# Scaling V's result instead of the probabilities in the first two attention chunks

## The chip, the cores and the metric

The kernel runs on one core of one Trainium2 chip. The metric is device time in microseconds (us) of one execution; a run is one timed execution. Three runs of the kernel before are shown, and one further execution was profiled.

## The reference

```python
scores = scale * np.matmul(q, k.transpose(0, 1, 3, 2))          # 4 batches, 8 heads, 768 positions, 64 per head
scores = scores - slope[h] * dist                               # distance bias; kept: 96 local keys, 8 global keys
scores = np.where(keep, scores, -1000000000.0)
a = np.exp(scores - np.max(scores, axis=-1, keepdims=True))
a = a / (np.sum(a, axis=-1, keepdims=True) + 1e-09)
x = np.matmul(a, v)                                             # heads side by side: 3072 tokens x 512
h = x @ w_in                                                    # 512 x 2048
g = 0.5 * h * (1.0 + erf(h / sqrt(2)))
out = g @ w_out                                                 # 2048 x 512
```

The weights come as 64-bit numbers, which the kernel takes apart itself.

## The kernel before

The 3072 tokens are 12 chunks `c` of 256 queries, three to a batch. A chunk first goes through the attention, 8 heads in 4 pairs `p`, then through 8 steps `s` of the two layers (256 of the 2048 inner columns each). Chunks 0 and 1 are interleaved: step 0 of chunk 0, three empty steps, then step 0 of chunk 1, step 1 of chunk 0, step 1 of chunk 1 and so on, while the weights of each step are still coming in; from chunk 2 on (`CAT`) the chunks follow each other. The list `EVENTS` says, for each chunk, at which step of the loop in `run` each part of its attention is written.

The attention of a pair of heads: `scores_pair` multiplies queries by keys on TensorE (tiles `s`) and VectorE adds the bias and finds the maximum (L358, tiles `n`); `exps` takes the exponential on ScalarE with the sum of each row (L379, `su`), VectorE adds 1e-9 and forms the reciprocal (L381, L382), and the probabilities are multiplied by it (L388; VectorE in chunks 0 and 1, GpSimd later). `flip` turns each head's probabilities by three transposes on TensorE (L398, tiles `t`), and ScalarE copies them to SBUF (L402, `pt`). `av_pair` multiplies by V (L430, `av`: per pair in chunk 0, per two pairs in chunk 1). The result goes to the tile `x` as a high part, a copy by ScalarE (L470, L475), and a low part, the rest, by VectorE (`lo_dve`, L177).

The layers: `m1` makes `h` (L506 for chunks 0 and 1; L489, L493, L495 later, with a sum of two halves on VectorE, L497). `gelu` reads it twice on ScalarE (`gh`, `gr`, L516, L517), and VectorE forms `gl` (L177). `m2` adds 12 products to `acc` (L536). The weights of a step are four pieces of 512 KB; each goes through ScalarE twice (L209, L229) and VectorE four times (L215, L217, L219, L177). In `run`, a step's `m1` stands ahead of the `m2` of the step before. `flag` gathers small checks near the end; it ends in a product on TensorE (L641, `flag_ps`) that waits for VectorE (`bad`, L639).

The exponential and the gelu need different function tables; a change of table is an `ACT_TABLE_LOAD` on ScalarE. `FILL` puts products with zeros (`warm`, L366) between the scores of chunks 0 and 1. The order on each engine is not that of the source: a scheduler, which follows data, buffers and the extra dependencies of `after`, lays the instructions out when the program is built, and each engine works through its list from the front.

Of the kernel before, what the change touches and what calls it, by code (L numbers as in the profile page):

```python
# [7 lines left out]
F32 = mybir.dt.float32  # L8
# [5 lines left out]
ALU = mybir.AluOpType  # L14
# [3 lines left out]
P = 128  # L18
# [3 lines left out]
NP = H // 2  # L22
# [19 lines left out]
EVENTS = [EVF, EVF, EVT] + [EVS] * (NCH - 3)  # L42
# [10 lines left out]
FILL = {(0, 0, 0): 8, (0, 0, 1): 5, (0, 1, 1): 9, (0, 2, 1): 4, (0, 3, 1): 4, (1, 0, 1): 4}  # L53
# [33 lines left out]
class Fast:  # L87
    def __init__(self, tc, ctx, qT, kT, v, w, out, limits):
# [22 lines left out]
        self.pt_n, self.pt_t, self.x = {}, {}, {}  # L111
# [4 lines left out]
    def consts(self):  # L116
# [3 lines left out]
        self.nmax = const.tile([P, 3 * NP + 1, 4], F32, name="nmax")  # L120
        self.qsc = const.tile([P, NP], F32, name="qsc")
# [198 lines left out]
    def scores_pair(self, c, p):  # L320
# [4 lines left out]
        su = self.sm.tile([P, 4], F32, name=f"su{c}_{p}", tag="su", bufs=4, padded_shape=[P, 8])  # L325
# [3 lines left out]
        prev = self.last_av if EVENTS[c] is not EVF else None  # L329
# [33 lines left out]

    def warm(self, n, prev=None):
# [7 lines left out]
    def exps(self, c, p):  # L372
# [9 lines left out]
        nc.vector.reciprocal(out=su, in_=su)  # L382
        if c >= 3:
            top = self.nmax[:, 3 * NP]
            nc.vector.tensor_tensor(out=top, in0=top, in1=mn, op=ALU.max)
        for nn, i in every:
            eng = nc.vector if c < 2 else nc.gpsimd
            ins = eng.tensor_scalar(out=nn, in0=nn, scalar1=su[:, i:i + 1], scalar2=0.0,  # L388
                                    op0=ALU.mult, op1=ALU.add)
        if c < 2:  # L390
            self.last_dve = ins.ins

    def flip(self, c, h):
        nc = self.nc
        nn = self.pt_n.pop((c, h))
        tp = self.bank([P, 3, P], f"t{c}_{h}")
        for i, o in enumerate((0, 2 * P, NK if c % CPB == 0 else P)):
            nc.tensor.transpose(tp[:, i, :], nn[:, o:o + P], self.ident)  # L398
# [6 lines left out]
    def av_pair(self, c, p):  # L405
# [15 lines left out]
        elif first:  # L421
            avb = self.bank([P, 2, n, P], f"av{c}_{p}")
            av = [avb[:, j] for j in range(2)]
        else:
            av = [self.bank([P, n, P], f"av{c}_{p}_{j}") for j in range(2)]
# [34 lines left out]
        if quarters:  # L460
# [6 lines left out]
            return  # L467
        if first:
# [9 lines left out]
    def m1(self, t, f):  # L478
# [5 lines left out]
        if c >= CAT:  # L484
# [3 lines left out]
            for d in range(NP):  # L488
# [3 lines left out]
                if d:  # L492
                    nc.tensor.matmul(hp[:, 0, :], lhsT=wl[:, d - 1, fs], rhs=x[:, d - 1, 0, :],  # L493
                                     start=False, stop=False, skip_group_check=True)
            nc.tensor.matmul(hp[:, 0, :], lhsT=wl[:, NP - 1, fs], rhs=x[:, NP - 1, 0, :],  # L495
                             start=False, stop=True, skip_group_check=True)
# [24 lines left out]
    def m2(self, t, k):  # L521
# [12 lines left out]
        for f in range(2):  # L534
            for g, w in ((gh, wh), (gh, wl), (gl, wh)):
                nc.tensor.matmul(acc, lhsT=g[:, f, ks], rhs=w[:, f, :],  # L536
                                 start=s == 0 and n == 0, stop=s == NST - 1 and n == 5)
# [284 lines left out]
```

## Time and profile before

| | us |
|---|---|
| three runs | 682.39, 683.29, 683.58 |
| median | 683.29 |
| the profiled execution's own time | 682.04 |
| its span (first to last instruction) | 680.2 |
| TensorE busy in the span | 665.6 |
| VectorE, ScalarE, GpSimd busy | 390.3, 364.6, 102.4 |

In the tables of rows, PE is TensorE's products and PEld its weight loads, DVE is VectorE, ACT ScalarE, POOL GpSimd. Names read as output<-inputs; tile numbers are left out there, so `t` is every `t0_0`, `t0_1` and so on (chunk, then head). A busy time of pipelined instructions includes the time that the last result takes to come out, so the spacing of starts tells the rate better.

### The profile page before, as it was taken

How to read it: one execution, taken by the hardware profiler on the slowest of the kernel's cores; microseconds unless marked ns; L12 is line 12 of the kernel's file. 1: busy time of each engine (PE TensorE's matmuls, PEld its weight loads, DVE VectorE, ACT ScalarE, POOL GpSimd, SP SyncE). 2: the span in 40 equal slices, each digit the busy share in tenths (PEclk: the TensorE clock that was granted, in tenths of full speed). 3: DMA queues.
4: the chain of work that ended last, by engine and by line, in shares of the span. 5: the costliest groups of instructions: out<-in, count | busy, mean ns of one | idle time of the engine just before them, and what ended most of it. 6: DMA issues, size and time to landing. Idle time of an engine off the chain costs nothing.

```text
span 680.2 us, 13571 instructions
## 1 busy us (share of the span) xinstructions
PE 665.6 (98%) x5215; PEld 561.5 (83%) x5215; DVE 390.3 (57%) x1136; ACT 364.6 (54%) x852; POOL 102.4 (15%) x232
## 2 busy tenths in 40 slices
PE   8989999999999999999999999999999999999996
PEld 6658898988888888888888888888888888888784
DVE  5989989334555654655555555555546555453432
ACT  3796687554654645536636537446456356363211
POOL 3100330310301301301201121031031031010000
PEclk9999999999999999999999999999999999999998
DMA  8945944241531613403514324224154052000001
GB/s 267 276 147 186 290 152 125 79 125 47 164 94 62 164 35 122 140 29 113 126 41 153 97 67 156 69 72 140 32 132 135 24 161 64 32 1 16 16 1 36
DMA packets 66183, 71.21 MB, mean 105 GB/s; under 512 B 32704, under 2 KB 49344, under 8 KB 66112
## 3 DMA queue, kind: packets, MB, share of 16 engines
q1 hardware_dynamic: 61664, 62.93, 30.6%
q10 hardware_dynamic: 4448, 7.34, 3.1%
q8 instruction: 43, 0.70, 0.4%
q14 instruction: 28, 0.23, 0.1%
HBM read 63.97 MB, written 6.29 MB: 103 GB/s over the span
## 4 chain that ended last, share of the span: by engine, by line
PE 94%; DVE 3%; ACT 2%; issue 0%; DVEq 0%
PE acc L536 40%; PE h L489 22%; PE h L493 8%; PE h L506 6%; PE av L430 5%; PE s L347 5%; PE t L398 4%; PE h L495 3%; PE warm_ps L366 1%; DVE n L358 1%; DVE n L388 1%; ACT w L209 0%; ACT n L379 0%; DVE wb L217 0%; ACT L516 0%
## 5 line engine op out<-in xcount | busy, mean ns | idle before, releaser
L489 PE MATMUL h<-x,winh 128*128 128x512 f32 x640 | 216.3, 400 | 0.0
L497 DVE TENSOR_REDUCE hs<-h 128x256 f32<-128x512 f32 x160 | 107.7, 685 | 99.5 <-PE h L495 98.9
L536 PE MATMUL acc<-wouth,gh 128*128 128x512 f32 x384 | 156.8, 408 | 2.2 <-ACT gh L516 2.2
L536 PE MATMUL acc<-woutl,gh 128*128 128x512 f32 x384 | 150.3, 392 | 0.0
L536 PE MATMUL acc<-wouth,gl 128*128 128x512 f32 x384 | 148.5, 393 | 0.1
L388 POOL TENSOR_SCALAR n<-n,su 128x192 f32<-128x192 f32 (+1 forms) x160 | 71.3, 464 | 438.3 <-ACT n L379 217.9
L177 DVE TENSOR_TENSOR gl<-gr,gh 128x512 fp32r<-128x512 f32 x96 | 67.5, 703 | 117.6 <-ACT gr L517 117.6
L493 PE MATMUL h<-x,winl 128*128 128x256 f32 x480 | 134.7, 281 | 0.0
L489 PEld LDWEIGHTS h<-x,winh 128*128 128x128 f32 x640 | 114.2, 188 | 20.4 <-issue 0.3
L516 ACT ACTIVATE gh<-hs 128x512 fp32r<-128x512 f32 x80 | 50.7, 633 | 125.6 <-DVE hs L497 122.1
L402 ACT COPY pt<-t 128x384 f32<-128x384 f32 x96 | 45.4, 479 | 112.8 <-PE t L398 109.5
L493 PEld LDWEIGHTS h<-x,winl 128*128 128x128 f32 x480 | 90.4, 188 | 7.2
L536 PEld LDWEIGHTS acc<-wouth,gh 128*128 128x128 f32 x384 | 72.2, 188 | 21.0 <-ACT xs L462 3.9
L536 PEld LDWEIGHTS acc<-wouth,gl 128*128 128x128 f32 x384 | 72.1, 188 | 17.0 <-issue 0.6
L536 PEld LDWEIGHTS acc<-woutl,gh 128*128 128x128 f32 x384 | 72.3, 188 | 12.3
L379 ACT ACTIVATE n<-n,mn 128x192 f32<-128x192 f32 (+1 forms) x144 | 62.3, 434 | 1.4 <-DVE mn L358 1.2
L358 DVE CUSTOM_DVE_ANT_0 n<-s,pen 128x192 f32<-128x192 f32 (+1 forms) x192 | 54.6, 340 | 2.2 <-PE s L347 2.2
L517 ACT ACTIVATE gr<-hs 128x512 f32<-128x512 f32 x80 | 49.3, 616 | 0.0
L506 PE MATMUL h<-x,winh 128*128 128x256 f32 x256 | 48.9, 286 | 0.4 <-ACT x L470 0.2
L398 PE MATMUL t<-ident,n 128*128 128x128 f32 x288 | 47.2, 274 | 1.2 <-DVE n L388 1.2
L430 PE MATMUL av<-pt,vr 64*64 64x64 f32 (+2 forms) x1312 | 42.8, 249 | 2.7 <-ACT pt L402 2.6
L495 PE MATMUL h<-x,winl 128*128 128x256 f32 x160 | 45.2, 282 | 0.0
(87 smaller groups left out, 738.2 us busy)
## 6 DMA issues: line engine op xcount, KB each, us to landing
w<-w SPq DMA_DIRECT2D x32, 512.0 KB, 5.0
c<-w SPq DMA_DIRECT2D x32, 512.0 KB, 5.3
out<-o ACTq DMA_DIRECT2D x23, 256.0 KB, 2.0
qr<-qT SPq DMA_DIRECT2D x11, 512.0 KB, 3.9
vr<-v SPq DMA_DIRECT2D x22, 256.0 KB, 4.2
kr<-kT SPq DMA_DIRECT2D x16, 320.0 KB, 5.0
vr<-v SPq DMA_DIRECT2D x19, 192.0 KB, 2.8
kr<-kT SPq DMA_DIRECT2D x36, 64.0 KB, 4.1
```

The costliest lines, as they stand in the source:

```text
L177: return self.nc.vector.tensor_tensor(out=out, in0=in_, in1=hi.bitcast(F32), op=ALU.subtract)
L358: ins = nc.vector.tensor_tensor_reduce(out=nn[:, j * NK:j * NK + n], in0=sp[hh][:, j, 0:n], in1=pen, scale=-slope(2 * p + hh), scalar=3e38 ...
L379: self.table(nc.scalar.activation(out=nn, in_=nn, func=AF.Exp, bias=mn[:, i:i + 1], scale=-1.0, accum_out=su[:, i:i + 1]))
L388: ins = eng.tensor_scalar(out=nn, in0=nn, scalar1=su[:, i:i + 1], scalar2=0.0, op0=ALU.mult, op1=ALU.add)
L398: nc.tensor.transpose(tp[:, i, :], nn[:, o:o + P], self.ident)
L430: ins = nc.tensor.matmul(out, lhsT=lhs, rhs=rhs, start=start, stop=stop, skip_group_check=True).ins
L489: nc.tensor.matmul(hp.rearrange("p e t -> p (e t)"), lhsT=wh[:, d, fs], rhs=x[:, d].rearrange("p e t -> p (e t)"), start=d == 0, stop=d == ...
L493: nc.tensor.matmul(hp[:, 0, :], lhsT=wl[:, d - 1, fs], rhs=x[:, d - 1, 0, :], start=False, stop=False, skip_group_check=True)
L495: nc.tensor.matmul(hp[:, 0, :], lhsT=wl[:, NP - 1, fs], rhs=x[:, NP - 1, 0, :], start=False, stop=True, skip_group_check=True)
L497: self.last_dve = nc.vector.tensor_reduce(out=self.h[t][:, f, :], in_=hp.rearrange("p e t -> p t e"), axis=mybir.AxisListType.X, op=ALU.ad ...
L506: nc.tensor.matmul(hp[:, f, :], lhsT=w[:, d, fs], rhs=x[:, d, e, :], start=n == 0, stop=n == 3 * NP - 1)
L536: nc.tensor.matmul(acc, lhsT=g[:, f, ks], rhs=w[:, f, :], start=s == 0 and n == 0, stop=s == NST - 1 and n == 5)
```

## The change

In chunks 0 and 1 the probabilities are no longer multiplied by the reciprocals. The transposes take the bare exponentials. After V's products, TensorE spreads the reciprocals of each head over that head's 64 rows: products of a reciprocal column, read 64 times, with the unit matrix (tile `r`, L490 of the changed file; four products of 64x128 for a pair of heads, 16 in each of the two chunks). ScalarE copies V's result out (`xs`), VectorE multiplies it by `r`, and then the high and low parts are made as before, from SBUF. V's products of chunk 0 are written one loop step later for pairs 0 to 2. `FILL` has 8 products of 512 columns fewer, and `FILL_T` adds two of 384 columns ahead of the transposes of head 6 of chunk 1. From chunk 3 on, a step's second layer has to stand behind the first layer of the next step.

```diff
@@ -39,7 +39,7 @@
-EVENTS = [EVF, EVF, EVT] + [EVS] * (NCH - 3)
+EVENTS = [EVF | {"av": (3, 4, 5, 5)}, EVF, EVT] + [EVS] * (NCH - 3)
...
-FILL = {(0, 0, 0): 8, (0, 0, 1): 5, (0, 1, 1): 9, (0, 2, 1): 4, (0, 3, 1): 4, (1, 0, 1): 4}
+FILL = {(0, 0, 0): 8, (0, 0, 1): 5, (0, 1, 1): 3, (0, 2, 1): 3, (0, 3, 1): 3, (1, 0, 1): 4}
+FILL_T = {(1, 6): 2}
+FILL_AV = {}
...
+        self.sums = const.tile([P, 2 * NP, 4], F32, name="sums")
...
-        su = self.sm.tile([P, 4], F32, name=f"su{c}_{p}", tag="su", bufs=4, padded_shape=[P, 8])
+        su = self.sums[:, c * NP + p] if c < 2 else self.sm.tile([P, 4], F32, name=f"su{c}_{p}", tag="su", bufs=4,
+                                                                 padded_shape=[P, 8])
...
-        prev = self.last_av if EVENTS[c] is not EVF else None
+        prev = self.last_av if c >= CAT else None
...
+    def zeros(self, n, out):
+        prev = self.last_t
+        for i in range(n):
+            ins = self.nc.tensor.matmul(out, lhsT=self.wz[:, 0:P], rhs=self.wz[:, 0:out.shape[1]],
+                                        start=True, stop=True, skip_group_check=True).ins
+            self.after(ins, prev, "behind the transposes of the head before")
+            prev = ins
...
         nc.vector.tensor_scalar(out=su, in0=su, scalar1=1e-9, scalar2=None, op0=ALU.add)
-        nc.vector.reciprocal(out=su, in_=su)
+        self.last_dve = nc.vector.reciprocal(out=su, in_=su).ins if c < 2 else self.last_dve
+        if c >= 2:
+            nc.vector.reciprocal(out=su, in_=su)
         if c >= 3:
             top = self.nmax[:, 3 * NP]
             nc.vector.tensor_tensor(out=top, in0=top, in1=mn, op=ALU.max)
+        if c < 2:
+            self.inv[c, p] = su
+            return
         for nn, i in every:
-            eng = nc.vector if c < 2 else nc.gpsimd
-            ins = eng.tensor_scalar(out=nn, in0=nn, scalar1=su[:, i:i + 1], scalar2=0.0,
-                                    op0=ALU.mult, op1=ALU.add)
-        if c < 2:
-            self.last_dve = ins.ins
+            nc.gpsimd.tensor_scalar(out=nn, in0=nn, scalar1=su[:, i:i + 1], scalar2=0.0, op0=ALU.mult, op1=ALU.add)
...
         tp = self.bank([P, 3, P], f"t{c}_{h}")
+        if (c, h) in FILL_T:
+            self.zeros(FILL_T[c, h], tp.rearrange("k i q -> k (i q)"))
         for i, o in enumerate((0, 2 * P, NK if c % CPB == 0 else P)):
-            nc.tensor.transpose(tp[:, i, :], nn[:, o:o + P], self.ident)
+            self.last_t = nc.tensor.transpose(tp[:, i, :], nn[:, o:o + P], self.ident).ins
...
+        if c < 2:
+            rb = self.bank([P, 2, n, P], f"r{c}_{p}")
+            for i, q in enumerate(ps):
+                su = self.inv.pop((c, q))
+                for j, hh in ((0, 0), (0, 1), (1, 0), (1, 1)):
+                    ins = nc.tensor.matmul(rb[hh * D:(hh + 1) * D, j, i, :], lhsT=dap(su, 2 * hh + j, [su.ap[0], [0, D]]),
+                                           rhs=self.ident, start=True, stop=True, skip_group_check=True).ins
+                    self.after(ins, self.last_av, "heads and halves in turn")
+                    self.last_av = ins
+            for j in range(n):
+                src, scale = (avb, rb) if first else (av[j], rb[:, j])
+                shape = [P, 2, n, P] if first else [P, n, P]
+                xs = self.pp.tile(shape, F32, name=f"xs{c}_{p}_{j}", tag="n")
+                if first:
+                    xh, xl = (self.x[c][:, ps.start:ps.stop, e].rearrange("d p (j q) -> d j p q", j=2) for e in range(2))
+                else:
+                    xh, xl = (self.x[c][:, ps.start:ps.stop, e, j * P:(j + 1) * P] for e in range(2))
+                nc.scalar.copy(xs, src)
+                nc.vector.tensor_tensor(out=xs, in0=scale, in1=xs, op=ALU.mult)
+                nc.scalar.copy(xh, xs)
+                self.lo_dve(xl, xs, xh)
+            return
...
-            nc.tensor.matmul(hp[:, 0, :], lhsT=wl[:, NP - 1, fs], rhs=x[:, NP - 1, 0, :],
-                             start=False, stop=True, skip_group_check=True)
+            self.last_m1 = t, nc.tensor.matmul(hp[:, 0, :], lhsT=wl[:, NP - 1, fs], rhs=x[:, NP - 1, 0, :],
+                                               start=False, stop=True, skip_group_check=True).ins
...
         for f in range(2):
             for g, w in ((gh, wh), (gh, wl), (gl, wh)):
-                nc.tensor.matmul(acc, lhsT=g[:, f, ks], rhs=w[:, f, :],
-                                 start=s == 0 and n == 0, stop=s == NST - 1 and n == 5)
+                ins = nc.tensor.matmul(acc, lhsT=g[:, f, ks], rhs=w[:, f, :],
+                                       start=s == 0 and n == 0, stop=s == NST - 1 and n == 5).ins
+                if n == 0 and c > CAT and self.last_m1[0] == t + 1:
+                    self.after(ins, self.last_m1[1], "behind the first layer of the next step")
                 n += 1
```

The lists of the engines change in three places that matter for what follows. In names such as `pt1_6` the first number is the chunk and the second the head; the last number is the buffer's.

The first place is ScalarE, from the second reading of chunk 0's first `h` (`gr0`) to the copies of the last transposed heads of chunk 1. Before:

```order
L379 ACTIVATE n1_5_629,su1_2_615<-n1_5_629,nmax_129 128x192 x2
L209 ACTIVATE w1_1_200<-w1_1_200 128x512
L402 COPY pt1_2_653<-t1_2_649 128x384
L402 COPY pt1_2_653<-t1_3_655 128x384
L229 CAST winh1_563<-wb1_0_568 128x512
L379 ACTIVATE n1_6_701,su1_3_690<-n1_6_701,nmax_129 128x192 x2
L379 ACTIVATE n1_7_704,su1_3_690<-n1_7_704,nmax_129 128x192 x2
L209 ACTIVATE w1_2_202<-w1_2_202 128x512
L402 COPY pt1_4_742<-t1_4_738 128x384
L475 CAST x1_614<-av1_1_0_660 128x2x128
```

And now:

```order
L212 ACTIVATE w1_1_201<-w1_1_201 128x512
L417 COPY pt1_2_643<-t1_3_645 128x384
L232 CAST winh1_558<-wb1_0_563 128x512
L502 COPY xs1_1_0_685<-av1_1_0_650 128x256
L502 COPY xs1_1_1_690<-av1_1_1_651 128x256
L504 CAST x1_609<-xs1_1_0_685 128x2x128
L504 CAST x1_609<-xs1_1_1_690 128x2x128
L417 COPY pt1_4_742<-t1_4_738 128x384
L391 ACTIVATE n1_6_705,sums_130<-n1_6_705,nmax_129 128x192
L417 COPY pt1_4_742<-t1_5_744 128x384
L391 ACTIVATE n1_6_705,sums_130<-n1_6_705,nmax_129 128x192
L391 ACTIVATE n1_7_708,sums_130<-n1_7_708,nmax_129 128x192 x2
```

The copies and casts of `x1`'s first half stood behind the exponentials of heads 6 and 7, and now stand ahead of them; one copy of `pt1_2` has moved ahead of `gr0`. Behind these exponentials both lists still have five weight pieces (`winh1`, `w1_2`, `w1_3`, `w2_0`, `w2_1`) ahead of the last copies, those of `pt1_6`.

The second place is TensorE, from the transposes of head 7 of chunk 1 to the first layer. Before:

```order
L398 MATMUL t1_7_776<-ident_132,n1_7_704 128x128 x2
L430 MATMUL av1_3_0_781<-pt1_4_742,vr1_191 64x128
L430 MATMUL av1_3_1_782<-pt1_4_742,vr1_191 64x128 x2
L506 MATMUL h4_827<-x1_614,winh0_322 128x256 x2
...
L506 MATMUL h5_876<-x0_342,winh1_563 128x256 x2
L430 MATMUL av1_3_0_781<-pt1_6_774,vr1_191 64x128
```

And now:

```order
L413 MATMUL t1_7_778<-ident_133,n1_7_708 128x128 x2
L447 MATMUL av1_3_0_783<-pt1_6_776,vr1_192 64x128 x2
L447 MATMUL av1_3_1_784<-pt1_6_776,vr1_192 64x128 x2
...
L490 MATMUL r1_3_809<-ident_133,sums_130 64x128 x8
L545 MATMUL h4_844<-x1_609,winh0_307 128x256 x2
```

Twenty-three of the 48 products of `h4` and `h5` stood ahead of V's products with `pt1_6`; now all 48 stand behind them and behind the spread reciprocals.

The third place is TensorE at the beginning of chunk 11. Before:

```order
L495 MATMUL h91_1_7249<-x11_6911,winl0_323 128x256
L536 MATMUL acc11_0_7330<-wouth0_324,gh91_7259 128x512
...
L536 MATMUL acc11_1_7337<-wouth0_324,gl91_7260 128x512
L641 MATMUL flag_ps_7297<-ident_132,bad_7295 1x128
L489 MATMUL h92_0_7304<-x11_6911,winh1_563 128x512 x2
```

And now:

```order
L534 MATMUL h91_1_7266<-x11_6928,winl0_308 128x256
L575 MATMUL acc10_0_6835<-wouth7_1454,gh90_7198 128x512
...
L575 MATMUL acc10_1_6843<-wouth7_1454,gl90_7199 128x512
L682 MATMUL flag_ps_7314<-ident_133,bad_7312 1x128
L528 MATMUL h92_0_7321<-x11_6928,winh1_558 128x512 x2
```

The 12 products of `acc10` stood in the middle of `h91` and now stand behind it; those of `acc11`, which need `gh91`, stood right behind `h91` and now stand behind `h92`. The product of the checks now comes ahead of them.

## Rows read from the trace of the kernel before

**Rows 1.** Busy us by engine and stretch, steady part: PE, PEld, DVE, ACT, POOL.

```profile
200.00:300.00 100.00, 100.00 (x768) 85.41 (x767) 55.12 (x171) 53.67 (x128) 17.58 (x40) 1.00 0.33 100
600.00:650.00 50.00, 48.50 (x304) 40.65 (x304) 20.03 (x43) 16.71 (x35) 3.28 (x8) 1.00 0.03 12
```

**Rows 2.** The same view, three stretches of the first two chunks.

```profile
10.44:37.91 27.47, 25.20 (x232) 17.75 (x231) 23.98 (x104) 22.22 (x72) 1.84 (x4) 1.00 0.96 303
37.91:51.00 13.09, 11.08 (x107) 7.22 (x105) 11.25 (x42) 12.71 (x34) 0.00 (x0) 1.00 0.28 88
12.25:31.17 18.92, 16.89 (x155) 11.40 (x151) 16.50 (x74) 14.67 (x50) 1.84 (x4) 1.00 0.93 281
```

**Rows 3.** Timeline, chunk 0: start, busy us, instruction, count, [idle before it].

```profile
13.20 0.94 DVE L388 TENSOR_SCALAR n<-n,su 128x128 f32<-128x128 f32 x4
...
18.80 0.41 PEld L430 LDWEIGHTS av<-pt,vr 128*64 128x64 f32 x6 [0.17 <-issue]
18.80 1.03 PE L430 MATMUL av<-pt,vr 128*64 128x128 f32 x14
...
19.38 0.31 PEld L430 LDWEIGHTS av<-pt,vr 64*64 64x64 f32 x8 [0.17 <-issue]
```

**Rows 4.** Timeline of ScalarE, from `gh0` to the last copies of chunk 1.

```profile
37.91 0.60 ACT L516 ACTIVATE gh<-h 128x512 fp32r<-128x512 f32 x1
38.41 0.59 ACT L517 ACTIVATE gr<-h 128x512 f32<-128x512 f32 x1
39.01 1.28 ACT L379 ACT_TABLE_LOAD   x1
...
42.62 0.84 ACT L402 COPY pt<-t 128x384 f32<-128x384 f32 x2
...
46.95 0.63 ACT L475 CAST x<-av 128x256 fp32r<-128x256 f32 x2
47.48 0.63 ACT L229 CAST winh<-wb 128x512 fp32r<-128x512 f32 x1
48.00 1.25 ACT L209 ACTIVATE w<-w 128x512 int32<-128x512 uint32 x2
49.15 0.47 ACT L402 COPY pt<-t 128x384 f32<-128x384 f32 x1
...
50.09 0.84 ACT L402 COPY pt<-t 128x384 f32<-128x384 f32 x2
```

**Rows 5.** Timeline of TensorE and VectorE, second half of chunk 1.

```profile
44.66 1.28 PE L430 MATMUL av<-pt,vr 128*64 128x128 f32 x38
...
58.39 0.28 PE L506 MATMUL h<-x,winl 128*128 128x256 f32 x1
...
55.58 0.75 DVE L177 TENSOR_TENSOR x<-av,x 128x256 fp32r<-128x256 f32 x2
```

**Rows 6.** Timeline of TensorE, then of VectorE, around the beginning of chunk 11.

```profile
629.68 0.27 PE L495 MATMUL h<-x,winl 128*128 128x256 f32 x1
631.40 0.50 PE L536 MATMUL acc<-wouth,gh 128*128 128x512 f32 x1 [1.45 <-ACT gh L516]
...
632.64 0.50 PE L536 MATMUL acc<-wouth,gl 128*128 128x512 f32 x1
...
624.53 0.23 DVE L635 CAST wmin<-wand 128x128 f32<-128x128 int32 x1
...
625.12 0.15 DVE L637 TENSOR_SCALAR ok<-mx 128x1 f32<-128x1 f32 x1
...
631.90 0.69 DVE L177 TENSOR_TENSOR gl<-gr,gh 128x512 fp32r<-128x512 f32 x1 [1.22 <-ACT gr L517]
...
632.81 0.16 DVE L639 TENSOR_REDUCE bad<-ok 128x1 f32<-128x5 f32 x1
```

**Rows 7.** The chain that ended last: start, us, instruction, count.

```profile
1.46 5.49 PE warm_ps L366 x12
...
60.63 2.86 PE h L506 x24
...
668.25 5.54 PE acc L536 x24
```

More of the change, by code (lines that the diff above doesn't have):

```diff
@@ L110, in __init__ @@
         self.kt, self.qt, self.vr, self.raw = {}, {}, {}, {}
-        self.pt_n, self.pt_t, self.x = {}, {}, {}
+        self.pt_n, self.pt_t, self.x, self.inv = {}, {}, {}, {}
         self.stat, self.g, self.h, self.acc = {}, {}, {}, {}
@@ L423, in av_pair @@
             av = [avb[:, j] for j in range(2)]
+            if (c, p) in FILL_AV:
+                self.zeros(FILL_AV[c, p], avb.rearrange("d j n q -> d (j n q)"))
         else:
```

## The prediction

> **What bounds the kernel now.** I read the stretches first, then the timeline where they are not full, then the chain. From 200 to 300 us TensorE is busy in all 100 us [rows 1]; the same holds for every stretch of 60 to 600 us, so nothing done there on another engine can show, and TensorE's work there is unchanged. What is left is the beginning and the one leak near the end, 48.50 of 50 us [rows 1]. So the prediction is the shift of the moment from which TensorE is full, plus what happens to that leak.
>
> In the beginning the reader is to see that no engine is full for the whole time. Up to 37.91 us, where chunk 0's first `h` is read, TensorE is busy for 25.20, VectorE for 23.98 and ScalarE for 22.22 of 27.47 us [rows 2]: a chain that passes from engine to engine. Between 37.91 and 51.00 it is ScalarE alone: 12.71 of 13.09 us [rows 2]. The scalings that are taken away are VectorE's; the copies that are added are ScalarE's, and the spreading products TensorE's.
>
> **Totals.** The 32 scalings cost 0.94 us for four [rows 3], 7.5 us of VectorE; eight products with `r` come instead, each about the size of a low part of `x`, 0.75 us for two [rows 5], so 3.0 us. VectorE is relieved by 4.5 us. ScalarE gets eight more copies of 256 columns, 0.53 us for two (46.95 to 47.48 [rows 4]), 2.1 us. TensorE gets 32 spreading products. Their nearest row is V's product of the same 64x128 shape: three take the 0.58 us from 18.80 to 19.38 less the 0.17 us of issue that a change of shape costs [rows 3], so 0.14 each; bounds are 0.19 (the 0.58 us undivided) and 0.07 (two running side by side). That is 32 x 0.14 = 4.5 us and some changes of shape. Against it stand eight zero products fewer at 5.54/24 = 0.23 us [rows 7], 1.85 us. The two new ones of 384 columns, 0.17 us each, lie in a wait (below).
>
> **Term A, up to the first gelu (37.91 us).** TensorE's list from 12.25 to 31.17 us is 16.89 us of work in 18.92 [rows 2]; the rest is waits for probabilities, which the change removes. The same list now has 1.85 less for the zeros, 1.03 more for V's last products of chunk 0 (they stood behind 31.17; fourteen take 1.03 [rows 3]), 16 x 0.14 + 4 x 0.17 = 2.9 more for the spreading, 0.2 less for fewer changes of shape, and 0.3 less for two run-outs before waits (a product's busy time of 0.28 [rows 5] against a spacing of 2.86/24 = 0.12 [rows 7]). That is 18.4 us without any wait, so this point comes 0.5 us sooner. The saved scalings are therefore mostly filled with new products. The other end is ScalarE: if it never waited, it would reach `gh0` after 22.22 us and 1.5 us of additions (four copies and one `pt` copy that moved ahead), at 34.2 instead of 37.91, 3.7 sooner. ScalarE waits for TensorE's transposes there, so I take a value near TensorE's end, and a little more because `h0` no longer has V's products in its middle: **-0.8 us** (from -3.7 to +0.3, the latter with spreading at 0.19).
>
> **Term B, from `gr0` to the last `pt1_6` copy.** This is where the new list costs. Before, it ran from 38.41 to 50.09 + 0.84 = 50.93: 12.5 us, nearly without a gap. Now ScalarE does `gr0`, the table, four exponentials and a weight piece as before, 42.62 - 38.41 = 4.2 us, and one `pt` copy (0.42) [rows 4]. Then TensorE, which has been waiting for that copy, does 19 of V's products (38 issues, 1.28 us [rows 5]), eight spreading products (8 x 0.14 + 0.17 = 1.3 us), VectorE two products with `r` (0.75 us [rows 5]), and ScalarE, with only two `xs` copies and a weight piece to do meanwhile, casts `x1` (0.27): 3.6 us. Behind the casts wait, in ScalarE's list, a `pt` copy, an exponential, a `pt` copy, three exponentials (four take 4.2 - 0.60 - 1.28 - 0.57 = 1.75), the weight piece `winh1` (0.52, 47.48 to 48.00), four pieces at 1.15/2 (48.00 to 49.15) and two `pt` copies (0.84) [rows 4]: 6.2 us. The sum is 4.2 + 0.4 + 3.6 + 6.2 = 14.4 us, so **+1.9 us**. Bounds: if the 3.6 us were wholly filled with other work of ScalarE, only the two `xs` copies less one `pt` copy would be left, +0.1; with spreading at 0.19, +2.3.
>
> **Term C, from there to the end of `h4`.** Before, 50.93 to 58.39 + 0.12 = 58.51: 7.6 us. Now V's products (1.28 less a run-out of 0.16), the spreading (1.3) and all 48 products of `h4` and `h5` at 0.12 come behind the copy: 1.1 + 1.3 + 5.7 = 8.1 us, **+0.5 us** (from 0 to +0.9 with the spreading's bounds). Before, 23 of the 48 filled TensorE's wait for the copy; the two added zero products are all that fills it now. From here on TensorE is full as before; VectorE's weight pieces, about 1 us later, were done several us ahead of their use.
>
> **Term D, chunk 11.** TensorE ends `h91` at 629.68 + 0.12 and stands until 631.40 for `gh91`, 1.6 us, and about 0.2 us more before 632.64 for `gl91` [rows 6]. With `acc10` (12 x 0.23 = 2.8 us) behind `h91` this hole closes. But the check product `flag_ps` now stands there and needs `bad`, which stands behind `gl91` in VectorE's list. From the last product of `h91` to the start of `gl91` took 631.90 - 629.68 = 2.2 us, from there to the end of `bad` 632.97 - 631.90 = 1.1 us, and three small operations (624.53 to 625.27, 0.7 us [rows 6]) now stand in front of it too: 4.0 us. The last product of `h91` moves to 626.9, so `bad` is there at 630.9, while TensorE is through with `acc10` at 629.8: a new stand of 1.1 us, with all of `h92` queued behind it. Net **-0.7 us** (from -1.8, no stand, to 0).
>
> The extra order between the layers elsewhere is hidden: in the full stretch any order costs the same work. The moved DMA issues of chunk 2 are needed tens of us later.
>
> **Sum.** -0.8 + 1.9 + 0.5 - 0.7 = +0.9 us. The profiled execution took 682.04 us, 1.84 more than its span of 680.2, so it would take 682.9. The median of the runs, 683.29, lies 1.25 above that execution; the same shift gives 684.2 us. A measurement of this kernel can tell about 0.2%, 1.4 us, from no change, so the likeliest case is no measurable change, on its slower side. Its own range is 682.9 to 685.8.
>
> **Rivals.** *The clock falls* (0.13). The first 12 zero products take 5.49 us, 0.46 each, against 0.23 later [rows 7]: TensorE ran at the lower of its two levels, 1.2 GHz, at the start, after having done nothing, and at 2.4 GHz later, although the clock column reads 1.00 throughout. In term B TensorE now stands some 6 us of 14, about 3 of them in one piece before the copies of `pt1_6`. If the level falls there, as many products as at the start run slow: 12 x (0.46 - 0.23) = 2.7 us, +3.6 in all, 686.9. For it speaks the longer stand; against it that before, with 2 us of standing between 37.91 and 51.00 [rows 2], `h` ran on at 0.12. The Trainium skill, "TensorE: Matmul & The Clock Gate", Part 1, "What's actually happening", says that the half rate is the default state, that activity releases it, and that an idle spell brings it back; the start of this trace agrees, and by that rule the stand would count against the change.
>
> *Spreading is dearer* (0.12). At 0.19 each, terms A, B and C grow by 1.1, 0.4 and 0.4: +2.8, 686.1. A unit matrix as the moving operand and a column read 64 times are not in the trace.
>
> *ScalarE runs through* (0.15), the other side. If the wait for VectorE, not TensorE's list, is what stops ScalarE up to 37.91, the 4.5 us taken from VectorE pass through to it, up to ScalarE's own floor: A is -3.7 instead of -0.8, the sum -2.0, 681.3: faster. For it speaks VectorE's 23.98 of 27.47 us; against it TensorE's 18.4 us of list. It decides once A is below -3.1.
>
> *The waits of B are filled* (0.12). If VectorE and TensorE are ready sooner than I think, B is +0.1 and the sum -0.9: 682.4, no measurable change, at the edge of faster.
>
> **How the numbers follow.** The forecast has 0.48: about 0.30 of it within 0.2%, 0.18 slower. Clock and spreading add 0.25 to slower; running through gives 0.15 to faster; filled waits 0.08 to the same and 0.04 to faster. Faster 0.19, same 0.38, slower 0.43. For eight in ten the range leaves out about half of the running through and of the clock's upper side: 681.3 to 686.9.
>
> **What would show it.** Right: `gh0` near 37.1 us; ScalarE's two casts of `x1` standing right behind a gap, ahead of head 6's exponentials; last `pt1_6` copy near 52; TensorE idle some 3 us before it; `h4` done near 59.4; a stand of about 1 us before `flag_ps` and none for `gh91`. Wrong: `gh0` before 35 us, or spreading products more than 0.19 apart, or `h` products 0.24 apart after the stand, or TensorE with holes after 60 us.

## The result and the profile after

The changed kernel takes 686.65 us (median of six runs, 684.87 to 688.51) where the kernel before, run beside it, takes 682.8: a ratio of 1.0053, interval 1.0041 to 1.0066. It is slower by about 3.9 us. The profiled execution took 687.53 us with a span of 685.8.

The stretches of the profile after come first (busy us of PE, PEld, DVE, ACT, POOL; then the granted clock).

```profile
45.00:50.00 5.00, 3.06 (x22) 1.79 (x20) 3.37 (x15) 4.65 (x16) 0.00 (x0) 1.00 0.22 89
50.00:55.00 5.00, 3.39 (x50) 2.86 (x52) 5.00 (x10) 3.47 (x8) 0.00 (x0) 0.66 0.30 93
55.00:60.00 5.00, 4.41 (x41) 4.04 (x39) 5.00 (x12) 3.26 (x9) 0.00 (x0) 1.00 0.68 241
60.00:65.00 5.00, 3.51 (x15) 3.31 (x16) 2.40 (x5) 1.23 (x1) 0.00 (x0) 0.68 0.79 265
...
600.00:650.00 50.00, 48.96 (x379) 41.40 (x372) 22.59 (x62) 20.41 (x44) 3.30 (x8) 1.00 0.03 12
```

From 45 to 65 us TensorE is busy for 14.4 of 20 us, and twice its granted clock falls to about two thirds of full speed in a slice: part of that time was spent at the level of 1.2 GHz. The stretch with the old leak [rows 1] is 0.46 us fuller than before.

Where the time went is read in the timelines. ScalarE first, the stretch of [rows 4]:

```profile
36.53 0.60 ACT L555 ACTIVATE gh<-h 128x512 fp32r<-128x512 f32 x1
37.03 0.59 ACT L556 ACTIVATE gr<-h 128x512 f32<-128x512 f32 x1
...
43.12 0.65 ACT L502 COPY xs<-av 128x256 f32<-128x256 f32 x2 [0.90 <-PE av L447]
44.63 0.74 ACT L504 CAST x<-xs 128x256 fp32r<-128x256 f32 x2 [0.86 <-DVE xs L503]
...
51.10 0.82 ACT L417 COPY pt<-t 128x384 f32<-128x384 f32 x2
...
56.35 0.63 ACT L502 COPY xs<-av 128x256 f32<-128x256 f32 x2
58.70 0.62 ACT L232 CAST winh<-wb 128x512 fp32r<-128x512 f32 x1 [1.72 <-DVE wb L222]
59.22 0.71 ACT L504 CAST x<-xs 128x256 fp32r<-128x256 f32 x2
```

Then TensorE, from V's products for `x1`'s first half to the first product of chunk 1's `acc`, and the product of the checks:

```profile
41.75 1.27 PE L447 MATMUL av<-pt,vr 128*64 128x128 f32 x38 [1.24 <-ACT pt L417]
42.96 1.09 PE L490 MATMUL r<-ident,sums 128*64 128x128 f32 x16
43.98 0.88 PE L351 MATMUL s<-kr,qr 64*64 64x192 f32 x16
...
51.61 2.55 PE L447 MATMUL av<-pt,vr 128*64 128x128 f32 x40 [2.28 <-ACT pt L417]
54.09 1.52 PE L490 MATMUL r<-ident,sums 128*64 128x128 f32 x16
55.53 0.50 PE L545 MATMUL h<-x,winh 128*128 128x256 f32 x2
...
59.98 0.38 PE L545 MATMUL h<-x,winh 128*128 128x256 f32 x1 [0.59 <-ACT x L504]
61.85 0.58 PE L545 MATMUL h<-x,winh 128*128 128x256 f32 x1 [1.49 <-DVE x L180]
...
65.36 0.28 PE L545 MATMUL h<-x,winl 128*128 128x256 f32 x1
66.32 0.50 PE L575 MATMUL acc<-wouth,gh 128*128 128x512 f32 x1 [0.69 <-ACT gh L555]
...
637.08 0.27 PE L682 MATMUL flag_ps<-ident,bad 128*1 128x128 f32 x1 [1.04 <-DVE bad L680]
```

The reader is to see two places. In these rows a product with V, a transpose and a spreading product count as two entries each: the eight products `r1_3` of TensorE's list are the row of x16. At 51.61 TensorE has stood for 2.28 us, and 40 entries of V's products then take 2.55 us, where 38 took 1.28 before [rows 5]. At 59.98 and 61.85 `h4` has to wait for the second half of `x1`, and the 17 products from 61.85 to 65.36 are 3.51/16 = 0.22 us apart instead of 0.12. VectorE shows why that half is late:

```profile
58.58 0.74 DVE L503 TENSOR_TENSOR xs<-r,xs 128x256 f32<-128x256 f32 x2
59.25 0.68 DVE L222 CUSTOM_DVE_ANT_0 wb<-w,wb 128x1024 uint16<-128x1024 uint16 x1
59.85 0.68 DVE L220 SCALAR_TENSOR_TENSOR wb<-w,wb 128x512 int32<-128x512 int32 x1
60.45 0.68 DVE L180 TENSOR_TENSOR winl<-wb,winh 128x512 fp32r<-128x512 f32 x1
61.05 0.75 DVE L180 TENSOR_TENSOR x<-xs,x 128x256 fp32r<-128x256 f32 x2
```

`x1` now passes ScalarE, VectorE, ScalarE, VectorE, and at each of them pieces of weights stand in between: the scalings and the low parts start 61.05 - 58.58 = 2.5 us apart. Of this 0.74 us is the scalings' own work; three operations on weights fill the rest on VectorE, while ScalarE has ended its casts at 59.22 + 0.71 = 59.93.

Added up: `gh0` comes 1.4 us sooner, the last `pt1_6` copy 1.0 later (51.92 against 50.93), the end of `h4` 7.0 later (65.48 against 58.51). From the first product of chunk 1's `acc` to the end it is 619.5 us, 1.3 less than before. That makes 5.6 us between these two executions. Between the medians it is 3.9, since the two executions lie on opposite sides of theirs.

### The profile page after: what moved, and what is told of

It reads as the page before. It is cut to its first block, busy times and chain, and to the rows that moved or that the text cites. A ratio compares the mean times of both kernels' runs of the same rounds, so it can differ in the third digit from the quotient of the medians.

```text
span 685.8 us, 13684 instructions
## 1 busy us (share of the span) xinstructions
PE 668.1 (97%) x5273; PEld 565.4 (82%) x5273; DVE 386.0 (56%) x1112; ACT 367.3 (54%) x860; POOL 105.1 (15%) x232
## 4 chain that ended last, share of the span: by engine, by line
PE 92%; DVE 3%; ACT 3%; issue 1%; ACTq 0%; DVEq 0%
PE acc L575 39%; PE h L528 22%; PE h L532 8%; PE h L545 6%; PE av L447 5%; PE s L351 5%; PE t L413 4%; PE h L534 3%; PE warm_ps L378 2%; ACT n L391 1%; ACT w L212 0%; DVE n L362 0%; DVE wb L222 0%; ACT pt L417 0%; DVE x L180 0%
## 5 line engine op out<-in xcount | busy, mean ns | idle before, releaser
L404 POOL TENSOR_SCALAR n<-n,su 128x192 f32<-128x192 f32 (+1 forms) x160 | 73.6, 479 | 437.6 <-ACT n L391 220.0
L532 PE MATMUL h<-x,winl 128*128 128x256 f32 x480 | 134.6, 280 | 0.0
L528 PEld LDWEIGHTS h<-x,winh 128*128 128x128 f32 x640 | 114.1, 188 | 20.2 <-issue 0.3
L545 PE MATMUL h<-x,winh 128*128 128x256 f32 x256 | 49.8, 291 | 2.1 <-DVE x L180 1.5
L545 PEld LDWEIGHTS h<-x,winh 128*128 128x128 f32 x256 | 42.0, 196 | 4.4 <-DVE x L180 1.7
```

The costliest lines, as they stand in the source:

```text
L404: nc.gpsimd.tensor_scalar(out=nn, in0=nn, scalar1=su[:, i:i + 1], scalar2=0.0, op0=ALU.mult, op1=ALU.add)
L528: nc.tensor.matmul(hp.rearrange("p e t -> p (e t)"), lhsT=wh[:, d, fs], rhs=x[:, d].rearrange("p e t -> p (e t)"), start=d == 0, stop=d == ...
L545: nc.tensor.matmul(hp[:, f, :], lhsT=w[:, d, fs], rhs=x[:, d, e, :], start=n == 0, stop=n == 3 * NP - 1)
```

## The experiments

Medians of 5 to 12 runs each. The runs come from several jobs, each with the kernel before beside it (682.45 to 682.97 us); the third column is the difference of the two medians in the same job, the interval that of the ratio to the kernel before there. Savings between kernels of different jobs are told by the third column.

| kernel | us | us over before | ratio |
|---|---|---|---|
| changed kernel | 686.65 | 3.85 | 1.0053 (1.0041 to 1.0066) |
| x1 first | 683.66 | 1.21 | 1.0017 (1.0009 to 1.0026) |
| zeros in the stand | 683.47 | 0.72 | 1.0008 (0.9998 to 1.0017) |
| both | 682.01 | -0.44 | 0.9991 (0.9982 to 1.0000) |
| both, flag later | 680.76 | -1.95 | 0.9973 (0.9964 to 0.9982) |
| before with the new layer order | 681.43 | -1.02 | 0.9986 (0.9976 to 0.9996) |
| the same, flag later | 680.30 | -2.41 | 0.9970 (0.9958 to 0.9982) |
| spreading in chunk 0 alone | 685.84 | 3.39 | 1.0043 (1.0029 to 1.0057) |
| spreading in chunk 1 alone | 686.05 | 3.08 | 1.0048 (1.0036 to 1.0060) |
| both, `r` of chunk 0 twice | 683.89 | 1.18 | 1.0017 (1.0006 to 1.0028) |
| both, casts later | 682.01 | -0.70 | 0.9990 (0.9980 to 1.0000) |
| no spreading, zeros at the start | 685.68 | 2.93 | 1.0044 (1.0027 to 1.0060) |
| no spreading, fewer zeros | 691.88 | 9.13 | 1.0113 (1.0094 to 1.0132) |

**The two places, one by one.** First, the second half of `x1` is laid out ahead of the later pieces of weights.

```diff
-                nc.scalar.copy(xh, xs)
-                self.lo_dve(xl, xs, xh)
+                cast, low = nc.scalar.copy(xh, xs), self.lo_dve(xl, xs, xh)
+            if (c, p) == (1, 3):
+                self.last_table, self.last_dve = cast.ins, low.ins
             return
```

> The changed kernel, with the second half of x1 (its high and low part) ordered ahead of the weight pieces that are written after it, on ScalarE and VectorE. The changed kernel's trace has TensorE standing 0.6 and 1.5 us at 59.98 and 61.85 us for x1, and h products at 0.21 instead of 0.12 us behind the stand. Theory 1 (x1 is late because it queues behind weight pieces, and the low clock behind it is a consequence of the stand): both stands go and the 17 h products behind them run at 0.12, together 2.5 + 1.6 = 4.1 us less than the changed kernel, about 682.6 us. Theory 2 (the clock level, once fallen at the 2.3 us stand before V's products with pt1_6, stays low by itself): only the stands go, 2.5 us less, about 684.2, and slow h products remain. If the late x1 costs nothing because something else is late as well: 686.6, no change.

The stands for `x1` are gone and so is the slow spell behind them, as theory 1 has it. That takes 2.6 us off the change's loss (3.0 between the medians themselves), less than the 4.1 of theory 1 and nearer to the 2.5 of theory 2. The other place is as it was, in stretch and timeline:

```profile
50.00:55.00 5.00, 4.05 (x56) 3.52 (x56) 4.96 (x10) 2.54 (x6) 0.00 (x0) 0.50 0.47 151
...
50.95 2.56 PE L447 MATMUL av<-pt,vr 128*64 128x128 f32 x40 [2.28 <-ACT pt L417]
53.43 1.97 PE L490 MATMUL r<-ident,sums 128*64 128x128 f32 x16
61.65 0.50 PE L576 MATMUL acc<-wouth,gh 128*128 128x512 f32 x1 [0.21 <-ACT gh L556]
```

Second, on top of it, 16 products with zeros stand in the wait before the `pt1_6` copies.

```diff
             av = [self.bank([P, n, P], f"av{c}_{p}_{j}") for j in range(2)]
+            if (c, p) == (1, 3):
+                self.zeros(16, av[0].rearrange("d n q -> d (n q)"))
```

> As the run with x1 first, and with 16 zero products of 256 columns (0.12 us each, 1.9 us) on TensorE between the transposes of head 7 of chunk 1 and V's products of the second half, where it stands 2.3 us for the copies of pt1_6. If standing is what lowers the clock, V's 40 products and the 16 spreading products behind it run at the full rate (1.28 and 1.1 instead of 2.55 and 1.5 us): 1.6 us less than with x1 first alone, about 681 us if x1 first gives 682.6. If the clock falls for another reason, the products stay slow and the time is that of x1 first alone, or up to 0.5 us more where the zeros delay the products behind them.

The clock keeps its higher level, and 1.65 us more come back:

```profile
50.00:55.00 5.00, 4.77 (x77) 3.94 (x77) 5.00 (x11) 2.88 (x8) 0.00 (x0) 1.00 0.51 152
...
47.91 2.16 PE L371 MATMUL av<-wz 128*128 128x256 f32 x16
...
50.88 1.65 PE L449 MATMUL av<-pt,vr 128*64 128x128 f32 x40 [0.23 <-ACT pt L417]
52.46 1.09 PE L492 MATMUL r<-ident,sums 128*64 128x128 f32 x16
60.18 0.50 PE L578 MATMUL acc<-wouth,gh 128*128 128x512 f32 x1 [0.69 <-ACT gh L558]
```

The zeros give no result that anything uses; what they change is the level at which V's products and the eight spreading products (16 entries, 1.09 us instead of 1.97) run. Third, the zeros alone, without the edit for `x1`:

> The changed kernel with the 16 zero products of 256 columns in TensorE's stand before V's products with pt1_6, and nothing pinned for x1. (The lists shift with it: x1's second half's copies and products with r come ahead of two and four weight operations.) Theory (late x1 and the low clock are two costs, and the zeros take away only the clock's): the granted clock stays at 1.00 from 45 to 60 us, V's products and the spreading take 1.6 us less, and a part of the wait for x1 stays; between the changed kernel's 686.65 and the 682.0 of both edits, near 683.5. Rival (the zeros alone do it): 682.0. Rival (the zeros do nothing without x1 first, since x1 is late anyway): 686 or more.

As expected. One stand for `x1`, 0.9 us at 58.45, is left, and the products behind it run at full speed. The two edits save 2.6 and 3.1 us alone and 4.3 together. The slow spell after 61.85 of the changed kernel goes with either of them. The zeros are no clean test of the clock alone, though: as the expectation says, they also moved `x1`'s second half ahead of some pieces of weights, so a part of the 3.1 us belongs to that. What the clock alone costs is the 1.65 us between the two kernels with `x1` first.

**The layers' order.** The kernel before with nothing new but the order of a step's second layer behind the next step's first.

> The kernel before with the new order of the two layers from chunk 3 on and nothing else. Theory: the start is untouched; the holes of 1.5 and 0.2 us before acc11 go and a stand of about 1.0 us before the product of the checks comes in their place: 0.7 us less than before, about 682.1 us. Rival: the order also costs or saves something in the full stretch (the changed kernel's trace from its first acc product of chunk 1 to the end is 1.3 us shorter than before's, so as much as 1.3 less: 681.5), or the new stand costs as much as the old (682.8).

It gains 1.0 us, between the theory's 0.7 and the rival's 1.3, with a stand of 1.07 us before `flag_ps`. The product of the checks was then written four steps later, in the mended kernel and in this one (`flag_end` is the last part of `flag`, from that product on):

```diff
-                self.flag(flag_i)
+                self.flag()
+            if T == last - 4:
+                self.flag_end(flag_i)
```

> As x1 first with zeros, but the product of the checks is written four steps later, so that it no longer stands ahead of h92. Theory (term D: TensorE stands 1.0 us before it, with all of h92 behind): 1.0 us less, 681.0. Rival: the wait moves on to gh91 or gl91 in acc11, which stand behind h92: no gain, 682.0.

> The kernel before with the new order of the layers and with the product of the checks four steps later; nothing of the start is changed. Theory: no stand of more than 0.2 us is left after 60 us, so 1.0 us less than the order alone (681.4): 680.4, 2.0 below the kernel before. Rival: as the order alone, 681.4.

Both gain, 1.5 and 1.4 us, and the stand is gone. The two results together also answer what the spreading itself is worth. With the spreading, both places mended, it is 680.76 us; without it 680.30, in the same job. Chunk 1's first `acc` product stands at 60.34 and 59.82 us in their profiles; counted from the first exponential (9.54 and 10.05 us) that is 50.8 and 49.8 us. The kernel without the spreading has the lowest median of all, and it keeps the old scalings.

**One chunk alone.** The spreading in chunk 0 alone, chunk 1's probabilities scaled as before.

```diff
-        if c < 2:
+        if c == 0:
             self.inv[c, p] = su
             return
```

> The changed kernel with the spreading in chunk 0 alone; in chunk 1 VectorE scales the probabilities as before. Theory (the loss is made by chunk 1's second half: its xs copies, products with r and casts lie in ScalarE's and VectorE's queues among weight pieces): gh0 stays at about 36.5 us, the last pt1_6 copy ends near 50, x1 is not waited for, and the time falls to 1.4 + 0.8 us below before, about 680.6. Rival (chunk 0's part, with its copies and fewer zero products, is what upsets the order behind it): the stands stay, and the time stays within 1.5 us of the changed kernel's 686.6.

The second `c < 2`, at the spreading itself, is changed alike, and the scalings of the other chunk are put back. The theory, that chunk 1's spreading makes the loss, fell. `gh0` came at 36.17 us as expected, and then TensorE stood:

```profile
46.48 0.67 PE L416 MATMUL t<-ident,n 128*128 128x128 f32 x3 [1.81 <-DVE n L404]
...
57.30 0.39 PE L548 MATMUL h<-x,winh 128*128 128x256 f32 x1 [1.82 <-ACT x L517]
58.88 0.58 PE L548 MATMUL h<-x,winh 128*128 128x256 f32 x1 [1.19 <-DVE x L180]
```

The same for chunk 1 alone, with `FILL` and `EVENTS` of before:

```diff
-        if c < 2:
+        if c == 1:
             self.inv[c, p] = su
             return
```

> The changed kernel with the spreading in chunk 1 alone; chunk 0's probabilities are scaled by VectorE as before, the zero products of the scores and chunk 0's steps stand as before, the new order of the layers stays. Theory (ScalarE's wait for V's products, the spreading and VectorE's product between the last readings of gh0 and the last pt1_6 copy is made by chunk 1's part, whatever chunk 0 does): gh0 near 38 us as before, the stretch from gr0 to the last pt1_6 copy near 14.9 us instead of 12.5, with the flag's order giving 1.0 back: 684.1 us or more, if the clock falls too 686. Rival (the wait comes from chunk 0's V products, which the change moves to later steps, not from chunk 1's part): the stretch stays near 12.5 us and the time is that of the layers' order alone, 681.4.

The time is the theory's upper one. The stretch from `gr0` to the last `pt1_6` copy, though, grew by only 0.9 us (38.96 to about 52.4), not 2.4. What the trace shows beside this are the stand before V's products, the lower level behind it (granted clock 0.50 in 50 to 55 us) and the two stands for `x1`:

```profile
51.33 3.41 PE L450 MATMUL av<-pt,vr 128*64 128x128 f32 x48 [2.44 <-ACT pt L420]
54.67 1.24 PE L493 MATMUL r<-ident,sums 128*64 128x128 f32 x16
...
60.15 0.38 PE L548 MATMUL h<-x,winh 128*128 128x256 f32 x1 [0.46 <-ACT x L507]
61.58 0.39 PE L548 MATMUL h<-x,winh 128*128 128x256 f32 x1 [1.05 <-DVE x L180]
```

Either half of the change alone costs nearly as much as both. So the loss is not a price per spreading product.

**The terms A and B.** Chunk 0's 16 spreading products twice over, in the mended kernel:

```diff
-                for j, hh in ((0, 0), (0, 1), (1, 0), (1, 1)):
+                for j, hh in ((0, 0), (0, 1), (1, 0), (1, 1)) * (2 - c):
```

> As x1 first with zeros, but with chunk 0's 16 spreading products issued twice (the second time into the same place, same values). In the trace 16 spreading products start within 1.1 us, 0.065 each, so 16 more are 1.0 us of TensorE. Theory of the prediction (up to the first gelu TensorE's list is the limit): gh0 comes 1.0 us later and the time is 1.0 us longer, 683.0. Rival (ScalarE or VectorE is the limit there, TensorE has slack): gh0 moves by less than 0.3 us and the time stays at 682.0.

It costs 1.6 us (1.9 between the medians themselves). From the first exponential to `gh0` it is 28.17 us instead of 26.21, and TensorE has no gap left from 10.44 to 37 us:

```profile
10.44:37.00 26.56, 26.56 (x286) 19.40 (x284) 20.65 (x89) 22.01 (x76) 2.79 (x4) 1.00 0.97 311
```

So TensorE's list sets `gh0`, as term A had it. The expectation took entries for products. The four spreading products of chunk 0's first pair are eight entries in the changed kernel (shown first) and 16 here (shown second):

```profile
18.29 0.66 PE L490 MATMUL r<-ident,sums 128*64 128x128 f32 x8
```

```profile
18.03 1.09 PE L492 MATMUL r<-ident,sums 128*64 128x128 f32 x16
```

Sixteen more products are 32 entries at 0.065 us, 2.1 us, and `gh0` came 2.0 us later: the list explains all of it. Further on, the zeros in the stand did not keep the clock in this profile. They ran at the lower level themselves, 3.36 us for the 16 instead of 2.16, behind no stand longer than 1.23 us:

```profile
50.00:55.00 5.00, 4.89 (x36) 4.40 (x36) 4.78 (x11) 4.34 (x10) 0.00 (x0) 0.66 0.04 6
...
50.40 3.36 PE L371 MATMUL av<-wz 128*128 128x256 f32 x16
```

Then the casts of `x1`'s first half, moved behind the exponentials of heads 6 and 7 (excerpt; what is held back here is written behind those exponentials):

```diff
+                if (c, p) == (1, 1):
+                    self.held.append((xh, xl, xs))
+                    continue
                 cast, low = nc.scalar.copy(xh, xs), self.lo_dve(xl, xs, xh)
```

> As x1 first with zeros, but the casts and low parts of x1's first half are ordered behind the exponentials of heads 6 and 7, as in the kernel before. Theory (term B: ScalarE loses time because these casts wait for VectorE ahead of the exponentials, 0.86 us idle in the trace, and VectorE's low parts, 0.76 us, stand ahead of the maxima that the exponentials need): the stretch from gr0 to the last pt1_6 copy shrinks from 14.9 to about 14.1 us, and the time by 0.8 us to 681.2. Rival: ScalarE's wait there is for TensorE (V's products, spreading, scores), so the casts only move and the stretch stays within 0.2 us: 682.0.

The median is the same: ScalarE now waits for TensorE's transposes instead, and the stretch from `gr0` to the last `pt1_6` copy takes 15.1 us.

```profile
44.80 0.48 ACT L421 COPY pt<-t 128x384 f32<-128x384 f32 x1 [1.61 <-PE t L417]
```

What was lost in B is the wait for TensorE's list, wherever the casts stand.

**The zero products of the kernel before.** Both are made from the best kernel, without spreading. The first has ten more zero products before chunk 0's last V products, the second three zero products instead of 9, 4 and 4, as in the change.

```diff
             av = [avb[:, j] for j in range(2)]
+            prev = self.last_t
+            for i in range(10 if (c, p) == (0, 3) else 0):
+                ins = nc.tensor.matmul(avb.rearrange("d j n q -> d (j n q)"), lhsT=self.wz[:, 0:P], rhs=self.wz[:, 0:CT],
+                                       start=True, stop=True, skip_group_check=True).ins
+                self.after(ins, prev, "behind the transposes of head 7")
+                prev = ins
```

> The kernel before with the new order of the layers and the later product of the checks (680.3, runs from 679.7 to 682.7), and 10 zero products of 256 columns on TensorE ahead of V's products of the last pair of chunk 0, where it stands 1.33 us (27.58 to 30.00 us in the trace of before). In that trace the clock stayed at full level behind this stand; in the traces of the new order alone and with the later check, whose lists are the same up to there, it fell to 0.55 for about 4 us. Theory (the spread of the kernel before over 3 us comes from this fall, in some executions): clock 1.00 in 30 to 34 us, runs within 1.5 us of each other, median 0.8 us lower, 679.5. Rival (the spread comes from elsewhere): same spread, 680.3 or a little more for the zeros.

```diff
-FILL = {(0, 0, 0): 8, (0, 0, 1): 5, (0, 1, 1): 9, (0, 2, 1): 4, (0, 3, 1): 4, (1, 0, 1): 4}
+FILL = {(0, 0, 0): 8, (0, 0, 1): 5, (0, 1, 1): 3, (0, 2, 1): 3, (0, 3, 1): 3, (1, 0, 1): 4}
```

> The kernel before with the new order of the layers and the later product of the checks (680.3), and with the fewer zero products of the changed kernel (3, 3, 3 instead of 9, 4, 4), nothing else of its start. It tells where the earlier first gelu of the changed kernel (1.3 us from the first exponential) comes from. Theory (from the scalings that are gone, the zeros only make room for the spreading): without the scalings gone the zeros lay in waits; the first gelu moves by less than 0.3 us and the time stays at 680.3, or grows where TensorE stands longer and its clock falls. Rival (from the zeros): first gelu 1.3 us or more sooner, and 679.0.

The ten zeros did what was expected at their place: granted clock 1.00 from 30 to 34 us, `gh0` 1.0 us nearer to the first exponential. But the lists moved, stands of 2.38, 1.81 and 1.19 us appeared at 46.70, 55.60 and 57.18, and the runs spread over 5.4 us instead of 3.0. Neither the theory nor the rival foresaw that. The fewer zeros cost 11.5 us: `gh0` comes 33.3 us behind the first exponential instead of 28.2, so the earlier `gh0` of the changed kernel doesn't come from the fewer zeros. There is a clock of 0.79 from 18 to 26 and of 0.57 from 34 to 42 us, and there are waits:

```profile
18.00:26.00 8.00, 6.13 (x42) 3.74 (x42) 7.27 (x28) 6.01 (x21) 2.51 (x4) 0.79 0.87 211
...
34.00:42.00 8.00, 8.00 (x57) 6.31 (x56) 6.22 (x28) 4.66 (x15) 0.00 (x0) 0.57 0.42 142
...
53.93 1.09 PE L398 MATMUL t<-ident,n 128*128 128x128 f32 x4 [4.13 <-DVE n L388]
...
64.58 0.39 PE L506 MATMUL h<-x,winh 128*128 128x256 f32 x1 [1.81 <-ACT x L475]
66.16 0.58 PE L506 MATMUL h<-x,winh 128*128 128x256 f32 x1 [1.20 <-DVE x L177]
```

In these two the spreading is absent, yet the same pair of stands for `x1` is there. All five kernels that show that pair (the changed one, each chunk alone, and these two) are at least 0.4% slower than before; none of the others that were timed shows it. In the changed kernel the pair comes from where the scheduler leaves the second half of `x1` among the weight pieces, since moving that half removes it. That the same holds for the other four, where quite different edits bring the pair, is likely from the rows but was not tested.

## Why the prediction was right and wrong

Its largest chance, slower (0.43), was right, and the range to 686.9 held the time. The number was not: 684.2 with its own range to 685.8 against 686.65, where no measurable change was called the likeliest case. Two of its own signs of being wrong came, `h` products 0.22 us apart behind a stand, where it names 0.24, and TensorE with holes after 60 us; `h4` was done at 65.5 us instead of 59.4.

**Term A** was right in kind: TensorE's list sets `gh0`. -0.8 was forecast, -1.4 measured. It isn't the spreading that was mis-sized: eight products, 16 entries, start 1.02 us apart from what follows them (42.96 to 43.98), 0.13 us each where the sum has 0.14. The sum charges 1.03 us for V's last products of chunk 0, which move ahead of `h0`, and gives back only 0.3 for their leaving its middle, where they stood before:

```profile
32.20 1.03 PE L430 MATMUL av<-pt,vr 128*64 128x128 f32 x14
```

With all of it given back, TensorE's end would come 1.5 us sooner instead of 0.5. This is worked out from the rows; no run tests it by itself.

**Term B**, +1.9 forecast, +2.4 measured: the waits stood where they were put, at 43.12 and 44.63, and a third, 0.34 us, at 46.20. This is where the gain of A is given back. But its length isn't the price of chunk 1's spreading alone: the stretch takes 13.4 us with the spreading in chunk 1 alone and 15.6 us (36.66 to 52.22) with it in chunk 0 alone, where chunk 1 spreads nothing. Counted from the first exponential, the last `pt1_6` copy ends at 41.5 us in the changed kernel, at 41.8 and 42.0 with chunk 0 and chunk 1 alone, and at 40.5 before, whether `gh0` came sooner or not.

**Term C** is the step that failed: +0.5 forecast, +6.0 measured. It says that the products of `h4` and `h5` come back to back behind V's products and the spreading, and that VectorE's weight pieces "were done several us ahead of their use". TensorE stood for no piece there; but `x1`'s second half stands in line with them. The scaling of V's result put one more passage through VectorE and one more through ScalarE between `av` and `x`. I priced their work (0.75 and 0.53 us) in the totals, but term C has neither this work nor the queue in front of it. Stands of 0.59 and 1.49 us followed. Moving that half ahead takes 2.6 us off, so this is shown. Of the 5.5 us that the term lacks, the `h` products make 4.2 (9.95 us from 55.53 to 65.48 instead of 5.7), about half of it the stands and most of the rest the lower level behind them. The remainder lies in V's products and the spreading, where the clock had fallen.

**The clock** was a rival with 0.13 and belongs to what happened: the level fell after the longest stand. The argument against it, that 2 us of standing before had left `h` at 0.12, compared several shorter waits with one of 2.28 us. Filling it took 1.65 us off with `x1` mended; the 3.1 without hold a part of `x1`'s place as well. That its time of 686.9 nearly met the result, and that the range held it, is partly chance: it had no stand for `x1` in it. The Trainium skill, "TensorE: Matmul & The Clock Gate", Part 1, "What's actually happening", has an idle spell bring the half rate back. The trace agrees as far as that, with 0.66 granted in 50 to 55 us behind the stand of 2.28 us; that the level also fell behind shorter stands is told at the end.

**Term D** was right: the wait for `gh91` is gone, `flag_ps` stands for 1.04 us (1.1 forecast), and the order alone is worth 1.0 us (0.7 forecast; where the other 0.3 come from is open).

**The other rivals** fell. Spreading costs what the sum has, 0.13 us a product, and isn't dearer. ScalarE doesn't run through, since TensorE's list holds `gh0`. The waits of B are not filled.

Why a change that frees VectorE gains nothing even when mended (0.6 and 0.5 us slower than the same kernel without spreading, with the flag early and late): taking the scalings away takes waits out of TensorE's list, but TensorE was nearly full there and got the new work. The 1.4 us of A are paid for by the 2.4 of B.

## What to carry to other kernels

When a scaling moves behind a product, count the passages that the result now makes through each engine, and look at what stands in each engine's list between two passages; the queue can cost more than the operations. Look for the longest single stand that a new order leaves TensorE, and fill it, because the products behind it may run at half rate; then time the result, since zeros in another place moved other work and cost 5.3 us. And test the companions of an edit apart: the order of the layers, which came along here, was the part worth keeping.

## What was not expected of the hardware

The same list can keep or lose the clock from one execution to the next. The kernel before and the one with the new layer order have the same lists on TensorE from the first exponential to 31 us, with a stand of 1.33 us that ends at 30.00 and at 29.65 us. From 30 to 34 us the profiled executions show, first before, then with the new order:

```profile
30.00:34.00 4.00, 4.00 (x46) 3.16 (x47) 4.00 (x18) 2.52 (x9) 0.00 (x0) 1.00 1.01 400
```

```profile
30.00:34.00 4.00, 4.00 (x32) 2.98 (x31) 4.00 (x16) 2.55 (x10) 0.00 (x0) 0.57 1.01 397
```

TensorE is busy throughout in both, with 46 entries in one and 32 in the other. Two more kernels have this list: with the spreading in chunk 1 alone the level stayed at 1.00 behind the stand, with the later product of the checks it fell to 0.57. Nor is a stand needed that is as long as the one of 2.28 us: here it was 1.33.

Each run lists its mean granted clock, and with the kernel before the time goes with it: of 35 runs in one job, the nine at 0.992 took 683.56 to 684.25 us, the nine at 0.997 took 681.65 to 682.56. The kernel before spreads over about 3 us, the mended ones, whose clock stays at 1.00 from 10 to 70 us in their profiles, over about 1.1. With the changed kernel it fits less well: five of its six runs list 0.993 or 0.994 and take 684.87 to 687.53 us. A small spread doesn't by itself mean the full level: the six runs with the spreading in chunk 1 alone spread over 1.1 us, all of them at 0.991 to 0.994. The one attempt to remove the fall at 30 us from the kernel without spreading, ten zeros at the start, moved other work. So that the clock makes the spread rests on the runs' clocks alone.

The beginning varies as well. The first 12 zero products take from 4.34 to 5.49 us in the fourteen profiles, and the first exponential starts between 9.41 and 10.45 us. Moments of different profiles are best counted from there.
